# A four-tap filter as diagonal matrix products, a new channel map, and a list scheduler that looks no operation ahead, in one fused two-layer kernel

## The chip, the cores and the metric

The kernel runs on one core of a Trainium2 chip. The metric is the device time of one execution in microseconds (us); less is better.

The engines are named as in the profile: PE is TensorE (matrix products; PEld is its loading of stationary operands), DVE is VectorE, ACT is ScalarE, POOL is GpSimd, SP is the engine that issues the transfers. L562 is line 562 of the kernel in question; the two kernels have different line numbers, so this table goes with all the profiles below:

| work | line before | line after |
|---|---|---|
| transposes of the convolution kernel h | L542 | L546 |
| transposes of k, and diagonal products | none | L561, L578 |
| first stage of the transform | L562 | L599 |
| second stage | L574 | L613 |
| inverse transform, two stages | L596, L608 | L636, L651 |
| MLP: input transposes, up, down products | L774, L787, L804 | L840, L853, L870 |
| evictions from PSUM on ACT, on DVE | L511, L512 | L519, L520 |
| elementwise products and sums on DVE | L501 | L509 |
| normalization on DVE, on ACT | L738, none | L799, L798 |

## The reference

Sequence length S = 2048, D = 512 channels, MLP width 1376, bfloat16.

```
def A(q, k, v, shift_k, ssm_k, ssm_D):
    k_shift[s, d] = sum over t of k_pad[s + t, d] * shift_k[d, 3 - t]     # 4 taps, causal
    kv = k_shift * v
    y  = causal convolution of kv with ssm_k, per channel, length 2048    # by FFT in the reference
    y  = y + kv * ssm_D
    return q * y
def B(x): return gelu(layernorm(x) @ w1 + b1) @ w2 + b2

x = q
x = x + A(layernorm(x), k, v, ...);  x = x + B(layernorm(x))
x = x + A(layernorm(x), k, v, ...);  x = x + B(layernorm(x))
```

The convolution y depends on k, v and the coefficients only, so it is computed once for both layers. What is left of each layer is pointwise products, normalizations and an MLP.

## The kernel before

The convolution is done by TensorE as a two-stage transform (products with constant matrices), pointwise products on VectorE, and a two-stage inverse. It is done in two halves of 1024 positions. Between them and behind them eight MLP blocks of 512 positions run, four of which (layers 1 and 2 of positions 0 to 1023) need only the first half of the convolution; the last four need the second half. So MLP matmuls of the first four blocks are the filler that keeps TensorE busy during the second half of the convolution.

Once in the first half and twice in the second, two transfers of 1 MB each exchange partitions 0 to 63 of an array in SBUF with partitions 64 to 127. Such a pair is called a swap below; the VectorE products that follow need it.

Everything is recorded as operations with estimated durations, and a list scheduler fixes each engine's order when the kernel is built (code is shortened here and below):

```
for e in free:                              # each engine
    ...
    first = min(got)                        # the op that can start earliest
    lim = first[0] + (self.LOOK * d if e != SP else 0.0)      # LOOK = 0.6; d: duration of first
    x = min((x for x in got if x[0] <= lim), key=...)         # the most urgent op that can start by lim
```

With LOOK = 0.6 an engine may pass over an operation that is ready and leave itself idle for up to 0.6 of that operation's duration, for one of higher priority.

The filter on VectorE, four times in each half, each operation on 128 partitions x 1024 elements:

```
def shift(w, hf):
    for j in range(3): tap(3 - j, t[j])             # multiply by a coefficient row
    tt(t[1], t[0], t[1], ALU.add); tap(0, t[0]); tt(t[2], t[1], t[2], ALU.add); tt(t[1], t[2], t[0], ALU.add)
    v = A(0, 128, VV[hf] + w * 16, [512, 8], [64, 8], [1, 16])
    tt(v, t[1], v, ALU.mult)
```

The first stage of the transform takes slices of k*v as stationary operand, 128 rows by 64 columns, with 64 elements between columns (`co = 64`); for h the columns lie side by side (`co = 1`):

```
stage1([(R_H0, 64, 1, 256)], C1, 0, range(8))                     # h:   go = 64, co = 1
stage1([(VV[0], 1, 64, 0)], R_SX, 0, range(2 * w, 2 * w + 2))     # k*v: go = 1,  co = 64
...
ins.append((ri, i, j, A(0, 128, o + (8 * d8 + i) * go, [co, 64]), A(0, 128, R_F + fo + 128 * ri, [1, 128])))
```

In an access pattern such as `[co, 64]` the first number is the step in elements, the second the count.

Of the kernel before, what the change touches and what calls it, by code (L numbers as in the profile page):

```python
# [40 lines left out]
class Op:  # L41
    __slots__ = ("i", "engs", "eng", "fn", "dur", "preds", "succ", "prio", "tile", "dma", "start", "end",
                 "pos", "inc", "waits", "val", "npred", "ready", "bytes", "base", "extra")


class Prog:
# [6 lines left out]
    LOOK = 0.6  # L53
# [130 lines left out]
    def schedule(self):  # L184
        ops = self.ops
        n = len(ops)
# [17 lines left out]
        free = {e: 0.0 for e in (PE, ACT, DVE, POOL, SP)}  # L204
# [9 lines left out]
        while done < n:  # L214
            best = None
            for e in free:
                te = max(free[e], 0.0)
                got = []
                for o in ready[e]:
                    if o.eng is not None:  # L220
                        continue
                    s = max(te, o.ready)
                    new = [x for x in o.tile if x.base is None]
                    if new:
                        pl = self._place(new, s)
                        if pl is None:
                            continue
                        s = pl[0]
                    got.append((s, -o.prio, o.i, o))
                cand = None  # L230
                if got:
                    first = min(got)
                    d = first[3].dur if isinstance(first[3].dur, (int, float)) else first[3].dur[e]
                    lim = first[0] + (self.LOOK * d if e != SP else 0.0)
                    x = min((x for x in got if x[0] <= lim), key=lambda x: (x[1], x[0], x[2]))
                    cand = (x[:3], x[3])
                if cand is None:
                    continue
                o = cand[1]
                d = o.dur if isinstance(o.dur, (int, float)) else o.dur[e]  # L240
                if best is None or (cand[0][0], cand[0][0] + d) < best[0]:
                    best = ((cand[0][0], cand[0][0] + d), e, o, cand[0][0])
# [18 lines left out]
            if o.dma:  # L261
                dma_free = max(dma_free, s + d) + o.bytes / 370.0
                o.end = dma_free + 1900.0
            else:
                o.end = s + d
# [168 lines left out]
def bass_interleave_layers__ssm_conv_h3__mixer_channel_mlp__prompt_kernel(  # L434
# [3 lines left out]
    NS = 192  # L438
# [26 lines left out]
    R_ID, R_F, R_D, R_B1, R_U, R_T2, R_SJ = (place(n) for n in (128, 512, 16, 16, 256, 2048, 2048))  # L465
# [7 lines left out]
    R_SX = R_XT  # L473
    R_SR = R_HT + 7168 - 2048
    HR = C6
    HT1 = C6 + 4096
    TM = [C6 + 4096, C4 + 4096]
    VV = [R_V, C4]
    XS = [R_X0 + s * 512 for s in range(8)] + [R_K + s * 512 for s in range(8)]
    YS = [R_V + s * 512 for s in range(8)] + [C3 + s * 512 for s in range(8)]  # L480
    M_B1, M_ST, M_MV, M_RS, M_HF = 0, 16, 16 + 96, 16 + 96 + 32, 16 + 96 + 32 + 16
# [37 lines left out]
    def load_h(hf):  # L519
        dma(A(0, 128, HR, [1024, 4], [1, 1024]), dr(A_ssm_k, hf * B, [2048, 128], [128 * 2048, 4], [1, 1024]), 1 << 20)  # L520

    def load_kv(hf):
        if hf == 0:
            dma(A(64, 64, R_K, [1, 1536]), dr(A_k, (8 * 64 - 3) * 512, [8 * 512, 64], [1, 1536]), 3 << 16)
            dma(A(1, 63, R_K, [1, 1536]), dr(A_k, 5 * 512, [8 * 512, 63], [1, 1536]), 3 << 16)
        else:
            dma(A(0, 128, R_K, [1, 1536]), dr(A_k, (B - 3) * 512, [8 * 512, 128], [1, 1536]), 3 << 17)
        dma(A(0, 128, R_K + 1536, [1, 4096]), dr(A_k, hf * B * 512, [8 * 512, 128], [1, 4096]), 1 << 20)
        dma(A(0, 128, VV[hf], [1, 4096]), dr(A_v, hf * B * 512, [8 * 512, 128], [1, 4096]), 1 << 20)
# [4 lines left out]
    def turn_h(hf, dst0):  # L534

        for a2 in range(2):
            tl = Tile(cv[hf], 0, hi[hf])
            ins = [(i * 512 + b * 128, A(0, 128, HR + b * 1024 + 4 * a2 + i, [8, 128])) for i in range(4) for b in range(4)]

            def f(e, ins=ins, tl=tl):  # L540
                for o, src in ins:
# [3 lines left out]
            evac(A(0, 128, dst0 + a2 * 32, [64, 64], [8, 4], [1, 8]),  # L545
                 lambda tl=tl: QB(tl, 0, 128, 0, [1, 64], [512, 4], [64, 8]), tl, dur={ACT: 1790.0, DVE: 2200.0})  # L546

    def stage1(terms, s, hf, d8s, engs=None):


        for d8 in d8s:
            tl = Tile(cv[hf], 0, hi[hf])
            ins = []
            for i in range(8):
                for j, (o, go, co, fo) in enumerate(terms):
                    for ri in range(2):
                        ins.append((ri, i, j, A(0, 128, o + (8 * d8 + i) * go, [co, 64]),
# [9 lines left out]
    def stage2(s, dst0, hf, g, engs=None):  # L567

        tl = Tile(cv[hf], 0, hi[hf])
        ins = [(i, A(0, 128, R_S2 + (16 * g + i) * 128, [1, 128]), A(0, 128, s + (16 * g + i) * 64, [1, 64])) for i in range(16)]  # L570

        def f(e):
            for i, w, m in ins:
                r = e.matmul(Q(tl, 0, 128, i * 64, [1, 64]), w, m, start=True, stop=True)  # L574
            return r
        P.op(PE, f, 16 * 29.0, reads=[x for y in ins for x in y[1:]], tile=tl)
        evac(A(0, 128, dst0 + 16 * g, [128, 64], [1, 16]), lambda: Q(tl, 0, 128, 0, [1, 64], [64, 16]), tl, engs)

    def swap(dst0, src0):
        for h in range(2):  # L580
            s = A(64 * h, 64, src0, [1, 8192])
            o = dma(A(64 - 64 * h, 64, dst0, [1, 8192]), s, 1 << 20, reads=[s])
        return o

    def G32(r, g):
        return A(0, 128, r + 32 * g, [128, 64], [1, 32])

    def inverse(p1, p2, z, y, hf):
        for d8 in range(8):
# [4 lines left out]
            def f(e, ins=ins, tl=tl):  # L594
                for i, j, w, m in ins:
# [3 lines left out]
            evac(A(0, 128, z + 8 * d8, [512, 16], [64, 8], [1, 8]),  # L599
                 lambda tl=tl: Q(tl, 0, 128, 0, [8, 16], [1, 8], [128, 8]), tl)  # L600
        for a2 in range(4):
            tl = Tile(cv[hf], 0, hi[hf])
            ins = [(i, ri, A(0, 128, R_T2 + ((2 * a2 + i) * 2 + ri) * 128, [1, 128]),
                    A(0, 128, z + ((2 * a2 + i) * 2 + ri) * 512, [1, 512])) for i in range(2) for ri in range(2)]

            def f(e, ins=ins, tl=tl):
                for i, ri, w, m in ins:
                    r = e.matmul(Q(tl, 0, 128, i * 512, [1, 512]), w, m, start=ri == 0, stop=ri == 1)  # L608
                return r
            P.op(PE, f, 4 * 216.0, reads=[x for y_ in ins for x in y_[2:]], tile=tl)  # L610
            evac(A(0, 128, y + a2 * 1024, [1, 1024]), lambda tl=tl: Q(tl, 0, 128, 0, [1, 1024]), tl)

    def shift(w, hf):  # L613

        t = [A(0, 128, TM[hf] + 1024 * i, [128, 8], [16, 8], [1, 16]) for i in range(3)]

        def tap(j, o):
            tt(o, A(0, 128, R_K + (3 - j) * 512 + w * 16, [512, 8], [64, 8], [1, 16]),
               A(0, 128, R_SJ + j * 512 + w * 16, [0, 8], [64, 8], [1, 16]), ALU.mult, 600.0)
# [6 lines left out]
        v = A(0, 128, VV[hf] + w * 16, [512, 8], [64, 8], [1, 16])  # L626
        tt(v, t[1], v, ALU.mult, 600.0)
# [4 lines left out]
    z = A(0, 1, R_K, [1, 1536])  # L632
    P.op(POOL, lambda e, z=z: e.memset(z, 0.0), 1300.0, writes=[z])
    tload(t_sm, row, 0, R_ID, 640)
    dma(A(0, 128, R_D, [1, 4]), dr(A_ssm_D, 0, [1, 128], [128, 4]), 1024)
    load_h(0)  # L636
    dma(A(0, 128, R_SR, [1, 2048]), dr(A_shift_k, 0, [0, 128], [1, 2048]), 1 << 19)
    load_kv(0)
# [4 lines left out]
    d0, dd = A(0, 128, HR, [1024, 4]), A(0, 128, R_D, [1, 4])  # L643
    P.op(POOL, lambda e: e.tensor_tensor(d0, d0, dd, ALU.add), 600.0, reads=[d0, dd], writes=[d0])
    for j in range(4):
        o, i = A(0, 128, R_SJ + 512 * j, [1, 512]), A(0, 128, R_SR + j, [4, 512])

        def f(e, o=o, i=i):
            if e is nc.scalar:
                return e.activation(o, i, AF.Copy)  # L650
            return e.tensor_copy(o, i)  # L651
        P.op((ACT, DVE), f, {ACT: 520.0, DVE: 600.0}, reads=[i], writes=[o])
    turn_h(0, R_H0)
    stage1([(R_H0, 64, 1, 256)], C1, 0, range(8))
# [9 lines left out]
    for w in range(4):  # L664
        shift(w, 0)
        stage1([(VV[0], 1, 64, 0)], R_SX, 0, range(2 * w, 2 * w + 2))
    for g in range(8):
        stage2(R_SX, C5, 0, g)
        if g % 2:
            tt(G32(C1, g // 2), G32(C5, g // 2), G32(C3, g // 2), ALU.mult, 1100.0)  # L670
            tt(G32(C4, g // 2), G32(C5, g // 2), G32(C4, g // 2), ALU.mult, 1100.0)
    inverse(C1, C4, R_SX, YS[0], 0)
# [4 lines left out]
    load_kv_late = load_kv  # L677
    load_h(1)
    load_kv_late(1)
    turn_h(1, HT1)  # L680
    stage1([(R_H0, 64, 1, 0), (HT1, 64, 1, 256)], C1, 1, range(8))
    for g in range(8):
        stage2(C1, C6, 1, g)
    for w in range(4):
        shift(w, 1)
        stage1([(VV[1], 1, 64, 0)], C1, 1, range(2 * w, 2 * w + 2))
# [13 lines left out]
    inverse(C6, C4, C1, YS[8], 1)  # L700
# [15 lines left out]
    def stats(sl, double):  # L716
# [13 lines left out]
        P.op(POOL, lambda e: e.tensor_scalar(v, v, m1, a1, ALU.mult, ALU.add), 220.0, reads=[v], writes=[v])  # L730
        h = M(0, 128, M_HF, [1, n])
        P.op(POOL, lambda e: e.tensor_tensor(r, v, h, ALU.pow), 1060.0, reads=[v, h], writes=[r])  # L732
        return [(M(0, 128, mv + 2 * i, [1, 1]), M(0, 128, M_RS + 4 * k + i, [1, 1])) for i in range(n)]

    def norm(s, mr, o):
        x = A(0, 128, XS[s], [1, 512])
        m, r = mr
        P.op(DVE, lambda e: e.tensor_scalar(o, x, m, r, ALU.subtract, ALU.mult), 350.0, reads=[x, m, r], writes=[o])  # L738
# [13 lines left out]
    for L, b in [(0, 0), (0, 1), (1, 0), (1, 1), (0, 2), (0, 3), (1, 2), (1, 3)]:  # L752
        lo = 2 if b < 2 else 0
        P.boost = {PE: 1e6, ACT: 2e6, DVE: 2e6, POOL: 2e6} if b < 2 else {}
        sl = list(range(4 * b, 4 * b + 4))
        mr = stats(sl, False)
# [6 lines left out]
        mr = stats(sl, True)  # L763
        k = blk[0]
        blk[0] += 1
# [79 lines left out]
```

## Time and profile before

302.0 us (median of four runs, 301.85 to 302.98). The profiled execution, one that took 300.4 us, has a span of 298.3 us at a mean granted TensorE clock of 0.949.

| | first half's convolution, 0 to 72.9 us | the rest, 72.9 to 298.3 us |
|---|---|---|
| TensorE busy | 43.5 us (60%) | 206.5 us (92%) |
| VectorE busy | 56.8 us | 149.9 us |
| granted clock | 0.86 | 0.98 |

I cut at the last eviction of the first half's inverse. The page first: busy totals, and the span in 40 equal slices (a digit is the busy share in tenths; PEclk is the granted clock in tenths).

```profile
PE 250.0 (84%) x2336; PEld 143.4 (48%) x2336; DVE 206.6 (69%) x407; ACT 155.4 (52%) x194; POOL 27.1 (9%) x43
...
PE   0788580795999999979899959995999999899995
...
PEclk9999756699999999999999997999699999999999
```

The stretches of the table, as the windows view of the kernel before gives them (length; busy of PE, PEld, DVE, ACT, POOL with instruction counts; clock; DMA share; GB/s):

```profile
0.00:72.90 72.90, 43.51 (x721) 39.23 (x722) 56.76 (x88) 41.57 (x41) 6.40 (x15) 0.86 0.77 255
72.90:298.30 225.40, 206.50 (x1616) 104.17 (x1616) 149.85 (x320) 113.83 (x153) 20.70 (x28) 0.98 0.13 34
```

The chain that ended last, its pieces in the first half (start, duration, what):

```profile
13.90 12.02 ACT ar L511 x13
...
30.07 2.41 DVE ar L501 x4
32.51 1.30 DVE ar L501 x2
...
45.18 9.17 DVE ar L501 x8
54.40 7.85 PE ps L596 x112
```

Read: evictions on ScalarE, then filter operations on VectorE, then eight VectorE products for which the whole inverse (L596) waits, TensorE idle. After that TensorE bounds the kernel.

TensorE's timeline just after the second half's inverse has ended at 200.0 us (the bracket is the idle time before the piece, and what ended it):

```profile
199.86 4.05 PE L804 MATMUL ps<-ar 128*128 128x512 bf16 x18
207.59 1.97 PE L774 MATMUL ps<-ar 128*128 128x128 bf16 x16 [3.67 <-DVE ar L738]
210.25 9.30 PE L787 MATMUL ps<-ar 128*128 128x512 bf16 x32 [0.69 <-ACT ar L511]
```

TensorE runs out of filler (L804), waits 3.7 us for the normalization that feeds the fifth MLP block, and then does 32 matmuls in 9.30 us; the same group takes 7.35 us at 254.5 us (granted clock 0.78 and 1.00 in the windows view of the two). This point, where the filler of the first four blocks ends and the fifth block begins, is called the handover below.

### The profile page before, as it was taken

How to read it: one execution, taken by the hardware profiler on the slowest of the kernel's cores; microseconds unless marked ns; L12 is line 12 of the kernel's file. 1: busy time of each engine (PE TensorE's matmuls, PEld its weight loads, DVE VectorE, ACT ScalarE, POOL GpSimd, SP SyncE). 2: the span in 40 equal slices, each digit the busy share in tenths (PEclk: the TensorE clock that was granted, in tenths of full speed). 3: DMA queues.
4: the chain of work that ended last, by engine and by line, in shares of the span. 5: the costliest groups of instructions: out<-in, count | busy, mean ns of one | idle time of the engine just before them, and what ended most of it. 6: DMA issues, size and time to landing. Idle time of an engine off the chain costs nothing.

```text
span 298.3 us, 5439 instructions
## 1 busy us (share of the span) xinstructions
PE 250.0 (84%) x2336; PEld 143.4 (48%) x2336; DVE 206.6 (69%) x407; ACT 155.4 (52%) x194; POOL 27.1 (9%) x43
## 2 busy tenths in 40 slices
PE   0788580795999999979899959995999999899995
PEld 0687570774855755344445424742335444344342
DVE  0699869799889936689889698749714777841031
ACT  1599542258899663552757231770451641654510
POOL 2100000221020000120220000301100110110000
PEclk9999756699999999999999997999699999999999
DMA  6997899730000059100005901000000000001001
GB/s 221 396 416 320 178 242 303 278 141 2 3 2 2 5 172 217 32 0 2 0 0 108 200 11 37 35 2 36 0 0 2 0 0 2 1 0 35 2 35 70
DMA packets 8753, 26.19 MB, mean 88 GB/s; under 512 B 2490, under 2 KB 3995, under 8 KB 7066
## 3 DMA queue, kind: packets, MB, share of 16 engines
q1 hardware_dynamic: 8730, 25.86, 28.1%
q8 instruction: 18, 0.29, 0.4%
q14 instruction: 5, 0.04, 0.0%
HBM read 17.47 MB, written 2.10 MB: 66 GB/s over the span
## 4 chain that ended last, share of the span: by engine, by line
PE 53%; DVE 18%; ACT 13%; DMA 10%; POOL 3%; issue 1%; SPq 1%; DVEq 0%
PE ps L804 17%; PE ps L787 17%; ACT ar L511 12%; DVE ar L501 10%; DMA ar<-ar 8%; PE ps L562 6%; PE ps L596 4%; PE ps L574 3%; DVE sm L724 3%; PE ps L774 2%; DVE ar L808 2%; PE ps L608 2%; DMA ar<-in_A_ssm_k_dram 2%; POOL sm L732 2%; DVE ar L738 2%; PE ps L542 2%
## 5 line engine op out<-in xcount | busy, mean ns | idle before, releaser
L511 ACT ACTIVATE ar<-ps 128x1024 bf16<-128x1024 f32 (+2 forms) x103 | 94.1, 969 | 70.9 <-PE ps L774 31.2
L501 DVE TENSOR_TENSOR ar<-ar 128x512 bf16<-128x512 bf16 (+2 forms) x160 | 102.8, 685 | 14.6 <-DMA ar<-ar 6.2
L792 ACT ACTIVATE ar<-ps,sm 128x512 bf16<-128x512 f32 (+1 forms) x88 | 60.4, 687 | 51.3 <-PE ps L787 51.0
L787 PE MATMUL ps<-ar 128*128 128x512 bf16 (+1 forms) x352 | 84.3, 387 | 3.2 <-ACT ar L511 2.1
L804 PE MATMUL ps<-ar 128*128 128x512 bf16 (+1 forms) x352 | 82.4, 385 | 3.9 <-DVE ar L808 3.9
L804 PEld LDWEIGHTS ps<-ar 128*128 128x128 bf16 (+1 forms) x352 | 33.0, 99 | 46.2 <-DVE ar L808 4.9
L787 PEld LDWEIGHTS ps<-ar 128*128 128x128 bf16 (+1 forms) x352 | 31.2, 101 | 48.9 <-ACT ar L792 15.1
L808 DVE TENSOR_TENSOR ar<-ar,ps 128x512 bf16<-128x512 bf16 x32 | 21.2, 685 | 43.2 <-PE ps L804 43.1
L724 DVE BATCH_NORM_STATS2 sm<-ar 128x6 f32<-128x512 bf16 x64 | 41.3, 681 | 0.0
L562 PE MATMUL ps<-ar 128*64 128x128 bf16 x640 | 31.4, 260 | 9.5 <-ACT ar L511 6.0
L562 PEld LDWEIGHTS ps<-ar 128*64 128x64 bf16 x640 | 29.1, 160 | 12.5 <-ACT ar L511 5.1
L738 DVE TENSOR_SCALAR ar<-ar,sm 128x512 bf16<-128x512 bf16 x64 | 23.0, 406 | 11.5 <-POOL sm L732 11.2
L730 POOL TENSOR_SCALAR sm<-sm 128x4 f32<-128x4 f32 x16 | 5.7, 357 | 224.8 <-DVE sm L726 224.8
L596 PE MATMUL ps<-ar 128*128 128x128 bf16 x256 | 16.9, 230 | 9.9 <-DVE ar L501 9.5
L574 PE MATMUL ps<-ar 128*128 128x64 bf16 x512 | 20.9, 202 | 5.0 <-ACT ar L511 2.9
L574 PEld LDWEIGHTS ps<-ar 128*128 128x128 bf16 x512 | 18.8, 104 | 10.9 <-ACT ar L511 7.2
L596 PEld LDWEIGHTS ps<-ar 128*128 128x128 bf16 x256 | 15.9, 104 | 11.2 <-DVE ar L501 9.6
L732 POOL TENSOR_TENSOR sm<-sm 128x4 f32<-128x4 f32 x16 | 18.1, 1130 | 1.3
L512 DVE CAST ar<-ps 128x1024 bf16<-128x1024 f32 x9 | 11.0, 1225 | 5.9 <-PE ps L574 2.5
L774 PE MATMUL ps<-ar 128*128 128x128 bf16 x128 | 10.4, 231 | 4.2 <-DVE ar L738 3.8
L542 PE MATMUL ps<-ar 128*128 128x128 bf16 x64 | 6.0, 269 | 8.7 <-DMA ar<-in_A_ssm_k_dram 7.1
L774 PEld LDWEIGHTS ps<-ar 128*128 128x128 bf16 x128 | 8.2, 103 | 7.2 <-DVE ar L738 5.0
(17 smaller groups left out, 38.6 us busy)
## 6 DMA issues: line engine op xcount, KB each, us to landing
ar<-ar SPq DMA_DIRECT2D x6, 1024.0 KB, 9.2
ar<-tab_s SPq DMA_DIRECT2D x4, 1024.0 KB, 16.1
ar<-in_A_ssm_k_dram SPq DMA_DIRECT2D x2, 1024.0 KB, 7.5
ar<-in_A_k_dram SPq DMA_DIRECT2D x2, 1024.0 KB, 8.3
ar<-in_A_v_dram SPq DMA_DIRECT2D x2, 1024.0 KB, 7.7
ar<-in_A_q_dram SPq DMA_DIRECT2D x2, 1024.0 KB, 13.4
out_dram<-ar SPq DMA_DIRECT2D x8, 256.0 KB, 2.2
ar<-in_B_w_dram SPq DMA_DIRECT2D x1, 1376.0 KB, 15.7
```

The lines of the kernel that those rows point to most:

```text
L501: return P.op(eng, lambda e: e.tensor_tensor(o, a, b, op), dur, reads=[a, b], writes=[o])
L511: return e.activation(dst, src(), AF.Copy)
L562: r = e.matmul(Q(tl, 64 * ri, 64, i * 128, [1, 128]), w, m, start=j == 0, stop=j == len(terms) - 1)
L574: r = e.matmul(Q(tl, 0, 128, i * 64, [1, 64]), w, m, start=True, stop=True)
L596: r = e.matmul(Q(tl, 0, 128, i * 128, [1, 128]), w, m, start=j == 0, stop=j == 1)
L724: P.op(DVE, lambda e, st=st, x=x: e.bn_stats(st, x), 630.0, reads=[x], writes=[st])
L738: P.op(DVE, lambda e: e.tensor_scalar(o, x, m, r, ALU.subtract, ALU.mult), 350.0, reads=[x, m, r], writes=[o])
L774: r = e.transpose(QB(tl, 0, 128, 128 * j, [1, 128]), src[j], IDN)
L787: r = e.matmul(Q(tl, 0, rows, 0, [1, 512]), w, m, start=dk == 0, stop=dk == 3)
L792: P.op(ACT, lambda e, dst=dst, tl=tl, rows=rows, bias=bias: e.activation(dst, Q(tl, 0, rows, 0, [1, 512]), AF.Gelu_apprx_tanh, bias=bias), ...
L804: r = e.matmul(Q(tl, 0, 128, 0, [1, 512]), ins[fc][0], ins[fc][1], start=fc == 0, stop=fc == 10)
L808: P.op(DVE, lambda e, x=x, tl=tl: e.tensor_tensor(x, x, Q(tl, 0, 128, 0, [1, 512]), ALU.add), 620.0, reads=[x], writes=[x], tile=tl)
```

## The change

Its intent is a shorter first half. Six parts come together:

- (a) In the first half, TensorE does the filter. It transposes k, and multiplies the shifted transposes by diagonal matrices of the coefficients, so that the product comes out in the original layout. VectorE only multiplies the result by v, out of PSUM.
- (b) The channel map is d = 8 g + j. Each group's 64 columns now lie side by side, so every stationary operand of the first stage is contiguous.
- (c) The first half's products and inverse are cut into two halves of channels, so that one half's inverse can run beside the other half's products. The second stage of k*v then runs as 256 matmuls of 32 columns.
- (d) The scheduler: LOOK is 0; a rule (PEN = 300) gives an operation that ScalarE or VectorE could do to VectorE only if ScalarE would be clearly later; two constants of its model change.
- (e) The MLP: normalizations may run on ScalarE (27 of 64 do), the second statistics of a block are computed for pairs, and earlier blocks get priority over later ones.
- (f) Loads: k first, in two pieces; the coefficients' spread for the second half moves to GpSimd.

```diff
-    LOOK = 0.6
+    LOOK = 0.0
+    PEN = 300.0
@@ scheduler
+                    if len(o.engs) == 2 and e == DVE:
+                        q = max(free[ACT], o.ready) + sum(... durations of more urgent ops ready for ACT ...)
+                        if q + o.dur[ACT] <= s + o.dur[DVE] + self.PEN:
+                            continue
@@ new: filter on TensorE, per block b of 128 channels
+        for a in range(8):
+            for j in range(4):
+                o = R_KT + (b * 8 + (a - j) % 8) * 132 + (2 if a >= j else 1)
+                ins.append((a, j, A(0, 128, o, [1, 128]), A(0, 128, R_DG + (b * 4 + j) * 128, [1, 128])))
+        ...     r = e.matmul(Q(tl, 0, 128, a * 128, [1, 128]), w, m, start=j == 0, stop=j == 3)
+        v = A(0, 128, VV[0] + b * 128, [512, 8], [8, 16], [1, 8])
+        o = A(0, 128, KV[0] + b * 1024, [8, 8], [64, 16], [1, 8])
+        P.op(DVE, lambda e: e.tensor_tensor(o, Q(tl, 0, 128, 0, [128, 8], [8, 16], [1, 8]), v, ALU.mult), ...)
@@ stage1
-                for j, (o, go, co, fo) in enumerate(terms):
-                        ins.append((ri, i, j, A(0, 128, o + (8 * d8 + i) * go, [co, 64]),
+                for j, (o, fo) in enumerate(terms):
+                        ins.append((ri, i, j, A(0, 128, o + (8 * d8 + i) * 64, [1, 64]),
@@ first half
-    for w in range(4):
-        shift(w, 0)
-        stage1([(VV[0], 1, 64, 0)], R_SX, 0, range(2 * w, 2 * w + 2))
-    for g in range(8): stage2(R_SX, C5, 0, g) ... products ...
-    inverse(C1, C4, R_SX, YS[0], 0)
+    stage1([(KV[0], 0)], R_SX, 0, range(8))
+    for u in range(2):
+        for g in range(4): stage2(R_SX, C5, 0, g, 32 * u, 32) ... products ...
+        inverse1(C1, C4, C6, 0, range(4 * u, 4 * u + 4))
+        inverse2(C6, YS[0], 0, 256 * u, 256)
@@ MLP
-        P.boost = {PE: 1e6, ACT: 2e6, DVE: 2e6, POOL: 2e6} if b < 2 else {}
+        first = (1e6, 2e6) if b < 2 else (0.0, 0.0)
+        P.boost = {e: first[e != PE] - 5e4 * k for e in (PE, ACT, DVE, POOL)}
-        mr = stats(sl, True)
+        mr = stats(sl[:2], True, k > 0) + stats(sl[2:], True, k > 0)
         ... (norm: DVE only before; ACT or DVE after)
```

## The prediction

> **What bounds the kernel now.** The table by stretches of the span (298.3 us) shows two regimes. Up to 72.9 us, the first half's convolution, TensorE is busy 43.5 us only. After that it is busy 206.5 of 225.4 us: TensorE-bound, with 19 us of holes. In the first regime the chain of waits runs through ScalarE's evictions (13.9 to 27 us, 1.03 us each), then VectorE filter multiplies (30 to 35 us), stage-2 evictions, eight VectorE products (45.2 to 54.4 us, TensorE and ScalarE idle) and the inverse transform (54.4 to 72.9 us). VectorE cannot evict from 12.7 to 35 us, because it runs 32 filter operations of 0.65 us (20.9 us in the timeline). TensorE's granted clock averages 0.64 from 30 to 55 us; [...] 128 stage-2 matmuls took 6.1 us there, against about 4.2 at full clock.
>
> **Removed.** The 32 filter operations on VectorE (20.9 us); the wait of the whole inverse for all eight products: channels now go in two halves, so the inverse of one overlaps the products of the other.
>
> **Added.** On TensorE, estimated from full-clock durations in the trace: 32 transposes (74 to 113 ns each, about 3 us), 128 diagonal matmuls (57 ns each in the second half's inverse, 7.3 us), and twice as many stage-2 matmuls for the k*v branch (33 ns each, so +4.2 us). On VectorE four multiplies out of PSUM (about 1.2 us each, like its 1.225 us evictions) and four diagonal builds (0.4 us). Eight short evictions.
>
> **New first half.** k lands near 6.5 us and TensorE starts before h is there; stage 1 starts near 12 us. TensorE then needs 5.6 + 7.3 + 4.2 + 5.6 + 8.4 = 31 us, so the inverse starts near 44. The new instruction order gives all its twelve evictions to ScalarE: 12 x 1.03 plus latency, so the first half ends near 58 us instead of 73.
>
> **The rest.** The second half's first transposes (2.4 us), done before 72.9 us today, move behind that point, so about 13 of the 15 us reach the end. The later part stays TensorE-bound. Some normalizations move to ScalarE (25-odd of 64 in the order), statistics come in pairs, and fewer holes should remain: I expect 3 to 5 of 19 us of holes, and of the two late clock dips (32 matmuls in 9.3 instead of 7.1 us at 210 us), to go.
>
> Predicted: 286 us (279 to 293). Faster by over 2%: 0.96; within 2%: 0.03; slower: 0.01.
>
> **What would show it.** Right: no vector filter operations in the first 45 us; first inverse matmul near 44 us, last first-half eviction near 58; granted clock near 1 from 15 to 55 us; TensorE busy about 260 us (250 + 14.5 - 4 from the clock). Holes after the first half: 14 to 16 us. Wrong: a gap before the first-half products, waiting for the partition-swap transfer (it must land by about 42 us); the clock still low; diagonal matmuls at over 70 ns.
>
> **What would make it wrong.** Evictions of the new layouts not at 1.03 us; the swap delayed by loads on the same queue; the scheduler's new order leaving TensorE without filler while second-half swaps (11.5 us each) run, which would give back 5 us; or filling the late holes better than I expect, which would bring 278 us.

The sum is 302 - 15 for the first part (58 for 73 us) - about 1 for the rest (2.4 us of transposes added, 3 to 5 us of holes taken off) = 286. That the clock of the new first half would be near 1 stands as my estimate, as does the line "- 4 from the clock", which is 6.1 - 4.2 and 9.3 - 7.1. The 4.2 and the 7.1 are estimates too, 128 matmuls at 33 ns and 32 at 0.22 us, from the matmuls of before at a clock of 1.00; measured there, a group of 32 takes 7.25 to 7.35 us.

## More of the kernel before

The group of first-stage matmuls (busy us, mean ns of one from start to end, idle before):

```profile
L562 PE MATMUL ps<-ar 128*64 128x128 bf16 x640 | 31.4, 260 | 9.5 <-ACT ar L511 6.0 <-DVE ar L501 3.3
```

## The result, and the profile after

277.2 us (median of four runs, 275.87 to 278.78). A ratio here is the mean time of one kernel's fast runs over the mean of the other's of the same rounds, so not quite the ratio of the medians: 0.9175, 95% interval 0.9112 to 0.9237. The direction was right; the time lies below the range of 279 to 293.

The profiled execution has a span of 277.0 us at a clock of 0.974. The same page lines and windows for the kernel after, cut at its own last first-half eviction, 62.9 us:

```profile
PE 244.4 (88%) x2640; PEld 144.8 (52%) x2640; DVE 183.4 (66%) x360; ACT 170.1 (61%) x221; POOL 45.6 (16%) x106
...
PE   0997953896999999988899899989999999989995
...
PEclk9999977899999999999799999999999999999999
```

```profile
0.00:62.90 62.90, 45.70 (x1006) 42.84 (x1007) 40.24 (x54) 38.77 (x42) 8.04 (x20) 0.92 0.88 290
62.90:277.00 214.10, 198.74 (x1637) 101.92 (x1635) 143.17 (x306) 131.38 (x179) 37.52 (x86) 0.99 0.14 35
```

So the span lost 21.3 us: 10.0 in the first part, where I had expected 15, and 11.3 in the rest, where I had expected about 1. TensorE has 304 instructions more and is busy 5.6 us *less*. In the rest, its busy time fell by 7.8 us and its idle time by 3.5 us (225.4 - 206.5 = 18.9, 214.1 - 198.7 = 15.4).

Over the whole kernel the busy time fell mainly in one group, the first stage, from 31.4 to 21.2 us. The new filter group and VectorE's product out of PSUM are beside it:

```profile
L599 PE MATMUL ps<-ar 128*64 128x128 bf16 x640 | 21.2, 220 | 2.9 <-ACT ar L519 2.8
...
L578 PE MATMUL ps<-ar 128*128 128x128 bf16 x128 | 8.0, 219 | 0.2 <-issue 0.2
...
L583 DVE TENSOR_TENSOR ar<-ps,ar 128x1024 bf16<-128x1024 f32 x4 | 4.9, 1225 | 7.5 <-PE ps L578 7.5
```

TensorE's waits, the two longest (line, what it waited for: us in total, times, longest), and its timeline in the first part:

```profile
PE ps L613 <- issue: 9.1, 3, 5.4
PE ps L561 <- DMA ar<-in_A_k_dram: 6.3, 1, 6.3
```

```profile
29.79 4.22 PE L599 MATMUL ps<-ar 128*64 128x128 bf16 x128
34.03 0.84 PE L613 MATMUL ps<-ar 128*128 128x32 bf16 x27
37.13 3.55 PE L613 MATMUL ps<-ar 128*128 128x32 bf16 x128 [2.25 <-issue]
46.06 2.88 PE L613 MATMUL ps<-ar 128*128 128x32 bf16 x101 [5.38 <-issue]
49.37 0.90 PE L636 MATMUL ps<-ar 128*128 128x128 bf16 x7 [0.43 <-issue]
```

The wait for the VectorE products, 9.5 us before, is gone. In its place stand holes that end at nothing the profile shows ("issue"): no operand, no semaphore, no buffer. The two long ones here fall in the middle of one uniform group of matmuls.

And the end of the second half's inverse (L651, over at 179.0 us), to be held against the three lines at 200 us of before:

```profile
178.80 1.89 PE L853 MATMUL ps<-ar 128*128 128x512 bf16 x8
181.98 6.23 PE L870 MATMUL ps<-ar 128*128 128x512 bf16 x28 [1.28 <-ACT ar L858]
188.05 1.06 PE L840 MATMUL ps<-ar 128*128 128x128 bf16 x16
189.70 2.50 PE L853 MATMUL ps<-ar 128*128 128x512 bf16 x10 [0.60 <-DVE ar L520]
```

Here 36 MLP matmuls are left to do while VectorE prepares the fifth block (35 of them start after the inverse has ended), and the block's transposes (L840) start without a hole. The same 16 transposes take 1.06 us, against 1.97 in before (clock 1.00 and 0.50 in the windows view).

### The profile page after: what moved, and what is told of

Read it like the earlier page. It is cut to its first block, busy times and chain, and to the rows that moved or that the text cites. A ratio compares the mean times of both kernels' runs of the same rounds, so it can differ in the third digit from the quotient of the medians.

```text
span 277.0 us, 6100 instructions
## 1 busy us (share of the span) xinstructions
PE 244.4 (88%) x2640; PEld 144.8 (52%) x2640; DVE 183.4 (66%) x360; ACT 170.1 (61%) x221; POOL 45.6 (16%) x106
## 4 chain that ended last, share of the span: by engine, by line
PE 61%; DVE 14%; ACT 9%; DMA 7%; issue 5%; POOL 2%; SPq 1%
PE ps L870 23%; PE ps L853 22%; ACT ar L519 6%; PE ps L613 5%; DVE ar L509 5%; DMA ar<-ar 5%; PE ps L636 4%; DVE ar L874 4%; PE ps L578 3%; DMA ar<-in_A_ssm_k_dram 3%; PE ps L599 2%; DVE ar L520 2%; DVE sm L776 2%; ACT ar L858 2%; ACT ar L798 1%
## 5 line engine op out<-in xcount | busy, mean ns | idle before, releaser
L509 DVE TENSOR_TENSOR ar<-ar 128x512 bf16<-128x512 bf16 (+2 forms) x132 | 85.1, 687 | 28.3 <-ACT ar L519 15.5
L858 ACT ACTIVATE ar<-ps,sm 128x512 bf16<-128x512 f32 (+1 forms) x88 | 59.2, 687 | 30.1 <-PE ps L853 29.8
L874 DVE TENSOR_TENSOR ar<-ar,ps 128x512 bf16<-128x512 bf16 x32 | 21.2, 685 | 38.1 <-PE ps L870 38.1
L782 POOL TENSOR_SCALAR sm<-sm 128x2 f32<-128x2 f32 (+1 forms) x24 | 7.9, 328 | 142.9 <-DVE sm L778 142.4
L613 PE MATMUL ps<-ar 128*128 128x64 bf16 (+1 forms) x640 | 21.5, 190 | 9.1 <-issue 9.1
L798 ACT ACTIVATE ar<-ar,sm 128x512 bf16<-128x512 bf16 x27 | 21.3, 811 | 4.7 <-POOL sm L789 4.7
L599 PE MATMUL ps<-ar 128*64 128x128 bf16 x640 | 21.2, 220 | 2.9 <-ACT ar L519 2.8
L799 DVE TENSOR_SCALAR ar<-ar,sm 128x512 bf16<-128x512 bf16 x37 | 14.4, 430 | 12.2 <-POOL sm L789 11.8
L599 PEld LDWEIGHTS ps<-ar 128*64 128x64 bf16 x640 | 18.4, 110 | 6.7 <-ACT ar L519 4.2
L787 POOL TENSOR_TENSOR sm<-sm 128x2 f32<-128x2 f32 (+1 forms) x24 | 21.4, 893 | 2.0
L636 PE MATMUL ps<-ar 128*128 128x128 bf16 x256 | 16.3, 225 | 0.7 <-issue 0.4
L520 DVE COPY ar<-ps 128x512 bf16<-128x512 bf16 (+1 forms) x20 | 9.6, 501 | 4.3 <-PE ps L561 2.4
L840 PE MATMUL ps<-ar 128*128 128x128 bf16 x128 | 9.6, 220 | 1.0 <-DVE ar L874 0.7
L840 PEld LDWEIGHTS ps<-ar 128*128 128x128 bf16 x128 | 7.8, 98 | 4.1 <-DVE ar L874 0.8
```

What stands on the lines that cost most here:

```text
L509: return P.op(eng, lambda e: e.tensor_tensor(o, a, b, op), dur, reads=[a, b], writes=[o])
L599: r = e.matmul(Q(tl, 64 * ri, 64, i * 128, [1, 128]), w, m, start=j == 0, stop=j == len(terms) - 1)
L613: r = e.matmul(Q(tl, 0, 128, i * nd, [1, nd]), w, m, start=True, stop=True)
L636: r = e.matmul(Q(tl, 0, 128, i * 128, [1, 128]), w, m, start=j == 0, stop=j == 1)
L787: P.op(POOL, lambda e: e.tensor_tensor(r, v, h, ALU.pow), 1060.0, reads=[v, h], writes=[r])
L798: return e.activation(o, x, AF.Identity, bias=mr[2], scale=mr[1])
```

## The experiments

Sixteen kernels ran. "After" and "before" are the two kernels above; times are medians, ratios are to the runs of before on the same chip in the same rounds. Theories:

- **T1**, mine at the start: the parts act where the prediction put them; what I missed in the rest is the first stage's contiguous operand.
- **R1**: the scheduler's order alone brings the gain, and the new operations little.
- **R2**: the filter and the channel halves bring nearly everything, the order little.

| kernel | us | ratio to before, 95% |
|---|---|---|
| sched_on_before | 301.2 | 0.998 (0.992 to 1.004) |
| order_mlp_on_before | 306.9 | 1.018 (1.013 to 1.023) |
| sched_off_after | 305.3 | 1.013 (1.009 to 1.017) |
| look_only | 306.0 | 1.013 (1.009 to 1.017) |
| look_pe | 290.7 | 0.962 (0.957 to 0.967) |
| look_dve | 297.8 | 0.984 (0.978 to 0.990) |
| pen_off | 293.7 | 0.971 (0.967 to 0.976) |
| norm_dve | 285.8 | 0.947 (0.941 to 0.953) |
| nosplit | 285.4 | 0.946 (0.940 to 0.953) |
| taps_dve | 283.9 | 0.942 (0.937 to 0.947) |
| strided_both | 298.6 | 0.993 (0.986 to 1.000) |
| strided_runs | 282.0 | 0.933 (0.929 to 0.937) |
| late_w | 276.6 | 0.914 (0.910 to 0.918) |
| late_w_again | 275.3 | 0.913 (0.909 to 0.917) |
| after_again | 276.4 | 0.916 (0.911 to 0.921) |
| tiny_swap (wrong result, one run) | 271.9 | none |

### Order or operations? sched_on_before, order_mlp_on_before, sched_off_after

The first puts part (d) alone on the kernel before, the second (d) and (e); the third takes (d) out of the kernel after.

```diff
sched_on_before, on before           sched_off_after, on after
-    LOOK = 0.6                      -    LOOK = 0.0
+    LOOK = 0.0                      -    PEN = 300.0
+    PEN = 300.0                     +    LOOK = 0.6
+ the rule for ScalarE/VectorE       - the rule
+ constants 700 and 400              + constants 0 and 370
```

> The kernel before with only the list scheduler's new rules (no look-ahead, ScalarE preferred for shared evictions, start and transfer constants). Theory 1 (the gain is in the work, not the order): the first half's chain still runs through 32 vector filter operations, so the time stays within 3 us of before, 299 to 303 us, and the last first-half eviction stays at 70 us or later. Rival (the new order is what fills the holes): 292 us or less, with holes on TensorE after the first half falling from 18.9 to under 14 us.

> The changed kernel with the old scheduler rules. Theory 1: 278 to 282 us, so at most 4 us of the 25 are the order's. Rival: 286 us or more.

> The kernel before with everything of the change that is not in the convolution: all scheduler rules, normalizations that may run on ScalarE, statistics in pairs, the priority of earlier MLP blocks. The changed kernel with the old rules took 305 us and the kernel before with the new rules 301 us, so either needs the other. If what is missing lies in the convolution's own operations (TensorE filter, map, halves): 296 to 304 us. If it lies in the MLP's operations: 285 us or less. In both cases the end of the second half's inverse plus 97 to 101 us gives the span, as in all ten runs so far.

Measured: with the operations of before, the new order gives 301.2 us against 301.5 for before in its rounds; with the MLP parts as well 306.9. With the operations of after and the old order 305.3. Only both together give 277.2. So neither R1 nor R2 holds: of the 25 us, none can be given to either alone. (306.9 lies above both ranges that I had written down for order_mlp_on_before.)

On before's operations the new order did shorten the rest (224.2 us from the end of the first half's inverse to the end, where before has 230.1) and lengthened the first part by more (that inverse ended at 75.9 us instead of 68.2). Why the first part lengthened I did not trace further. With the old order on after's operations, TensorE's busy time stays at 249.5 us even with a few records missing, five more than in after, and its holes over 0.15 us sum to 49.4 us against 28.8.

### Which part of the order? look_only, look_pe, look_dve, pen_off

All four are the kernel after with one thing put back: LOOK = 0.6 for all engines, for TensorE's list alone, for VectorE's list alone; or the ScalarE rule taken out.

```diff
look_only:  -    LOOK = 0.0
            +    LOOK = 0.6
look_pe:    -  lim = first[0] + (self.LOOK * d if e != SP else 0.0)
            +  lim = first[0] + (0.6 * d if e == PE else 0.0)
look_dve:   +  lim = first[0] + (0.6 * d if e == DVE else 0.0)
pen_off:    -  if len(o.engs) == 2 and e == DVE: ... continue      (the rule)
```

> The changed kernel with the old look-ahead of 0.6 of an operation's duration, all other rules new. The changed kernel with all old rules took 305 us: the eight first-half products stood in one block behind evictions, and the second half's second swap was issued at 163 us instead of 131 us. If the look-ahead is what does it: 298 to 306 us and the second swap issued after 155 us. If it is the rule that keeps shared evictions on ScalarE: 275 to 281 us.

> The changed kernel without the rule that keeps shared evictions and normalizations on ScalarE unless VectorE would be well ahead; no look-ahead, as in the change. If the look-ahead is what does it: 276 to 282 us. If the ScalarE rule does it: 295 us or more.

> The changed kernel with the old look-ahead of 0.6 of an operation on TensorE's list alone. With look-ahead on all engines it took 306 us, with 47 holes of 0.15 to 2 us (22 us) against 24 (15 us). If the loss is TensorE leaving ready filler matmuls for a more urgent operation that comes later than planned: 292 us or more. If it is VectorE's and ScalarE's order: 277 to 286 us.

> The changed kernel with the old look-ahead on VectorE's list alone. If VectorE's order (products kept behind more urgent MLP operations that are not yet ready) is what lengthens the second half's chain: 290 us or more, and the second half's inverse ends at 190 us or later. If it is TensorE's look-ahead: 277 to 284 us.

Measured, above after's 277.2: look-ahead on every list +29 us, on TensorE's alone +13, on VectorE's alone +21, the rule out +17. The parts do not add up. All four leave the operations as they are, so this is order alone. look_only and look_dve came as one of the two theories written down for each had it; look_pe (292 or more) and pen_off (295 or more) fell just short of theirs.

Where it goes is seen in two places. One is many small holes: TensorE has 47 holes of 0.15 to 2 us in look_only (22.3 us), 44 in look_pe (19.2 us) and 24 in after (14.9 us), counted in the traces. The other is the point at which the second half's inverse ends. These are TensorE's two longest waits in look_only; the second, 8.1 us, is the input transposes (L840) waiting for a normalization, which after's waits have with 0.2 us only:

```profile
PE ps L613 <- issue: 8.8, 3, 5.2
PE ps L840 <- DVE ar L799: 8.1, 3, 5.3
```

And TensorE's timeline in pen_off, where the last MLP matmuls (L864) run among the inverse's (L645):

```profile
190.25 1.89 PE L645 MATMUL ps<-ar 128*128 128x512 bf16 x8
191.97 0.81 PE L864 MATMUL ps<-ar 128*128 128x512 bf16 x3
200.50 1.89 PE L834 MATMUL ps<-ar 128*128 128x128 bf16 x16 [7.72 <-DVE ar L793]
203.08 10.12 PE L847 MATMUL ps<-ar 128*128 128x512 bf16 x32 [0.69 <-ACT ar L513]
```

The filler is spent when the inverse ends. TensorE waits 7.7 us for the fifth block's normalization, and afterwards runs at a reduced clock: the window view of pen_off has 0.70 from 200.5 to 215 us and 1.00 behind that. A second loss follows the hole: 32 matmuls take 10.1 us instead of the 7.35 seen in before at a clock of 1.00. That the hole is what brings the clock down is not shown by a run of its own. Counted over the traces in which all 704 MLP matmuls were recorded:

| kernel | MLP matmuls of the first four blocks that start after the second inverse has ended | longest hole after it, us |
|---|---|---|
| after, strided_runs, nosplit, late_w | 35 | 1.3 |
| before | 17 | 3.7 |
| look_only | 5 | 5.3 |
| pen_off, norm_dve, order_mlp_on_before | 2 | 7.7, 7.0, 7.7 |

look_dve (8.1 us), sched_off_after (5.4) and sched_on_before (6.6) show the hole too, but some matmul records are missing from their traces, so they are not counted. look_pe does not have it there; it loses by a 4.4 us hole at 110 us and by small ones. So one thing that most losing orders share is shown: filler used up before the handover to the fifth block. What is not shown by an experiment of its own is how much of each loss it makes. In pen_off the hole, less after's 1.3, and the slower 32 matmuls come to 6.4 + 2.8 = 9.2 of 16.5 us.

The hole is not the whole of it, for the traces show a rival to this reading. From the end of the second half's inverse to the end of the span, before takes 98.3 us, after 98.0, look_only 99.0, norm_dve 98.8 and pen_off 100.9 (look_pe alone is far from this, 106.6): a kernel that has used up its filler has less left to do, and the hole stands in its place. By this count the time is lost before the handover: that inverse ends at 179.0 us in after, 185.7 in norm_dve, 192.1 in pen_off, 195.0 in look_dve, 200.0 in before and 206.4 in look_only. The work that leads up to it runs late too: from the landing of the second half's first swap to the issue of its second, while its VectorE products run, after takes 14.5 us, norm_dve 18.0, pen_off, look_dve and look_only about 27 and before 38.0. The expectation of look_dve had named this chain, with an end of the inverse at 190 us or later as its mark, and the mark was met. But this stretch alone does not set the time: taps_dve has 26.6 us there and nosplit 25.0, and they lose 6.7 and 8.3. Either a late chain used up the filler, or an order that spent the filler early left the hole; no run separates the two, so the cause inside the order stays open.

### Normalizations on ScalarE, statistics in pairs: norm_dve

```diff
-        mr = stats(sl, False, k > 0)
+        mr = stats(sl, False, False)
-        mr = stats(sl[:2], True, k > 0) + stats(sl[2:], True, k > 0)
+        mr = stats(sl, True, False)
```

> The changed kernel with all normalizations on VectorE and statistics in fours, as before; filter, map, halves and scheduler stay. If relief of VectorE is what lets the eight products after the second half's first swap run at once (15.6 us from its landing to the second swap's issue, against 38.4 us before): 283 to 290 us and that stretch over 22 us. If it is the order alone: 276 to 280 us, stretch under 20 us.

Measured: 285.8 us, 8.6 more than after. What I expected between the second half's two swaps did not come: from the landing of the first to the issue of the second it took about 18 us. The hole is at the handover again:

```profile
185.57 0.81 PE L870 MATMUL ps<-ar 128*128 128x512 bf16 x3
193.37 1.98 PE L840 MATMUL ps<-ar 128*128 128x128 bf16 x16 [6.98 <-DVE ar L799]
196.03 10.09 PE L853 MATMUL ps<-ar 128*128 128x512 bf16 x32 [0.69 <-ACT ar L519]
```

7.0 us of hole and 10.09 - 7.35 = 2.7 us of slower matmuls (clock 0.76 from 194 to 210 us) are 9.7 us, against after's 1.3 us hole: 8.4 us, where the profiled span grew by 7.6 and the median by 8.6. That the part pays by keeping VectorE from being what TensorE waits for at this one point fits these lines, but is not shown: as said above, the inverse also ended 6.7 us later than in after.

### The two halves of channels: nosplit

```diff
-    for u in range(2):
-        for g in range(4): stage2(R_SX, C5, 0, g, 32 * u, 32) ...
-        inverse1(C1, C4, C6, 0, range(4 * u, 4 * u + 4)); inverse2(C6, YS[0], 0, 256 * u, 256)
+    for g in range(8): stage2(R_SX, C5, 0, g) ...
+    inverse1(C1, C4, C6, 0, range(8)); inverse2(C6, YS[0], 0)
```

> The changed kernel without the two channel halves in the first half: stage 2 of k*v in 64-column matmuls (128 instead of 256), all eight products, then the whole inverse. Theory: without the overlap the inverse starts 2 to 4 us later, but 128 fewer instruction pairs take one 16 KB block and its wait away, so the first half's inverse ends within 3 us of 61.6 us; 277 to 283 us. Rival (the halves are worth what the prediction thought): 284 us or more.

Measured: 285.4 us, 8.3 more than after, so the rival that put it at 284 or more was right. The wait that part (c) was meant to take away is back, one hole in TensorE's timeline:

```profile
51.40 9.48 PE L636 MATMUL ps<-ar 128*128 128x128 bf16 x128 [11.22 <-DVE ar L509]
```

The first half's inverse ends at 65.7 us instead of 61.6. That is as much as half of the 8.3 us. A hole of 4.3 us at 124.8 us, which after does not have, is as large as the other half; where it comes from I did not trace.

### The filter back on VectorE: taps_dve

This is the kernel after with the filter of the first half on VectorE, in the new layout (`shift(w, 0)` in place of the transposes and the diagonal products, with before's order of loads, and the coefficients' spread back on ScalarE and VectorE; so part (f) is undone with it).

> The changed kernel with the first half's filter back on VectorE (32 vector operations, k with its halo rows, no transposes of k, no diagonal matmuls); channel map, halves, scheduler and normalizations stay. Theory 1 (the filter on TensorE is worth about the 10 us by which the first half ended earlier, less what the map gives): 282 to 287 us, last first-half eviction at 67 to 71 us. Rival (the split into channel halves and the map gave nearly all of it): under 280 us.

Measured: 283.9 us, 6.7 more than after. TensorE waits for the filter in two places:

```profile
34.42 1.92 PE L599 MATMUL ps<-ar 128*64 128x128 bf16 x32 [4.54 <-DVE ar L509]
...
40.08 1.92 PE L599 MATMUL ps<-ar 128*64 128x128 bf16 x32 [3.74 <-DVE ar L509]
```

Yet the first half's inverse ends only 1.9 us later, at 63.5 us, and its last eviction at 64.7, where I had expected 67 to 71. In after the diagonal products end sooner, and the time goes into the holes without a cause at 35 and 41 us. So taking out the part for which the change is named, with (f), costs 6.7 us of the 25, and only 1.9 of it in the part it was meant for.

### The contiguous stationary operand: strided_both, strided_runs

Both give the first stage of k*v a stationary operand with 64 elements between columns again, as in before, and have VectorE write k*v in that layout.

```diff
-   A(0, 128, o + (8 * d8 + i) * 64, [1, 64])
+   A(0, 128, o + (8 * d8 + i) * go, [co, 64])       # k*v: go, co = 1, 64
strided_both: -  o = A(0, 128, KV[0] + b * 1024, [8, 8], [64, 16], [1, 8])
              +  o = A(0, 128, KV[0] + b * 16, [512, 8], [1, 16], [64, 8])     # neighbours 64 apart
strided_runs: +  o = A(0, 128, KV[0] + b * 16, [512, 8], [64, 8], [1, 16])     # runs of 16; its inputs are read with a step of 8
```

> The changed kernel, the order of all engines unchanged; only the filtered product k*v is stored so that the 64 columns of the stationary operand of its stage-1 matmuls lie 64 elements apart, as before, instead of side by side. Theory 1 (the channel map pays by contiguous weight loads): those 256 matmuls go from about 31 to about 66 ns, TensorE is busy 8 to 9 us longer, the second half's 4.5 us reach the end whole and the first half's in part: 282 to 286 us. Rival (the 66 ns were the clock's or the interleaving's doing, the map only rearranges): 276 to 279 us.

> Repeats the strided test without its fault: in the first one VectorE's scattered writes took 4.86 us each instead of 1.2. Here the product is written in runs of 16 elements; the stationary columns still lie 64 elements apart, the order of all engines is that of the changed kernel. Theory 1 (the map pays by contiguous weight loads): stage-1 matmuls of k*v at about 66 instead of 31 ns, TensorE busy 8 to 9 us longer in sum, time 281 to 286 us. Rival (the 21 us of the first test were VectorE's writes alone): 279 us or less.

strided_both came to 298.6 us, but it tells little of TensorE: VectorE's writes with 64 elements from each to the next cost 4.9 us each, not 1.2 (this line is its product out of PSUM, after's is shown above with a mean of 1225 ns):

```profile
L583 DVE TENSOR_TENSOR ar<-ps,ar 128x1024 bf16<-128x1024 f32 x4 | 18.7, 4857 | 5.1 <-PE ps L578 5.1
```

I had made the experiment without thinking of the writer. strided_runs mends most of that: VectorE writes in runs of 16 elements and reads every eighth, and the instruction order of every engine is that of after. It took 282.0 us, 4.8 more than after:

```profile
L602 PE MATMUL ps<-ar 128*64 128x128 bf16 x640 | 29.8, 248 | 3.4 <-ACT ar L519 2.5 <-DVE ar L877 0.6 <-DVE ar L520 0.3
...
L583 DVE TENSOR_TENSOR ar<-ps,ar 128x1024 bf16<-128x1024 f32 x4 | 8.1, 2027 | 4.7 <-PE ps L578 4.7
```

```profile
30.02 8.12 PE L602 MATMUL ps<-ar 128*64 128x128 bf16 x128
```

The same 128 matmuls took 4.22 us in after: 63 ns against 33 ns each. The group goes back to 29.8 us from 21.2, of before's 31.4. VectorE's products still cost 2.0 instead of 1.2 us, so not all of the 4.8 us is TensorE's, but the 8.6 us of matmul time is. TensorE's whole busy time rose by 5.6 us only (250.0 against 244.4): 2.5 of the 3.0 us between are two groups that ran at a reduced clock in after, the first 80 matmuls of the inverse (5.61 us at 0.84; 4.78 here) and 32 at 133.2 us (8.89 us at 0.81; 7.26 here). The mean clock is 0.994 here against 0.974. T1's missing term is shown. T1's other half, that the parts act where the prediction put them, is not borne out: taken out one at a time they cost 29 us (look_only), 17 (pen_off), 8.6 (norm_dve), 8.3 (nosplit) and 6.7 (taps_dve), far more than 25 in sum.

In the rest of the kernel the first stage took 16.8 us in before, 13.0 in after and 17.7 here. The windows view, of these matmuls alone (length; busy of PE and PEld; clock; DMA share; GB/s), first before, then after:

```profile
72.90:298.30 225.40, 16.82 (x384) 15.46 (x384) 0.98 0.13 34
62.90:277.00 214.10, 13.03 (x384) 11.09 (x384) 0.99 0.14 35
```

The remaining 1.6 of the 10.2 us saved are not the stride's: h's first 128 matmuls, contiguous in both kernels, took 5.57 us in before and 3.97 in after. Why is not shown; in after TensorE had started on k before them.

The number of columns is 64 in both layouts, and the time per matmul with its load still goes from 33 to 63 ns. For VectorE's product out of PSUM the three layouts measured are: 1.225 us with reads and writes in runs of 8 elements, 2.027 us with reads that step by 8 and writes in runs of 16, and 4.857 us with reads in runs of 8 and every element written 64 from the last.

### The holes without a cause: late_w, tiny_swap, after_again, late_w_again

What the trace of after shows: the holes that end at nothing stand after TensorE's 221st, 348th, 603rd and 731st matmul, 127, 255 and 128 apart. (A fifth, of 0.43 us after the 832nd, stands where a new group begins and does not fit the step.) The page's line for the instruction queue has 20 packets, 0.33 MB in all, 16 KB each. TensorE resumes 1.3 to 1.6 us after such a packet has landed: packets that land at 35.55 and 44.73 us, matmuls again at 37.13 and 46.06. In quiet stretches a packet starts when TensorE is at about the 85th matmul of a block of 128; up to 49 us it starts some 48 to 134 matmuls later than that, and the three long holes come where it is 106, 130 and 134. The packet itself takes 0.9 to 1.0 us before these holes, and 0.9 to 1.5 elsewhere: it starts late, it is not slow. That a packet feeds about 128 matmuls with their loads, a block, is my estimate from these distances and from the pages: 2640 matmuls, as many loads and 20 packets in after, 2336 and 18 in before, and 19 packets in nosplit, which has 128 matmuls fewer than after. The three long holes cost TensorE 9.1 us; from 34.9 to 49.4 us, where two of them end, the share of the DMA engines is 0.95. The theory: the packets queue behind the large transfers of the first half. late_w takes load from that time, moving the MLP weights behind the second half's v; tiny_swap does so as well, and cuts the first partition swap (2 MB within SBUF) to 1/16, with the rest of its target cleared by GpSimd, so its result is wrong.

```diff
late_w:     the three loads of w1 and w2 placed behind the load of v in SP's list; nothing else moved
tiny_swap:  the same, and
-   o = dma(A(64 - 64 * h, 64, dst0, [1, 8192]), A(64 * h, 64, src0, [1, 8192]))
+   o = dma_start(A(64 - 64 * h, 64, dst0, [1, 512]), A(64 * h, 64, src0, [1, 512]))
```

> The changed kernel, the order of all compute engines unchanged; only the loads of the two MLP weights (2.8 MB) go behind the second half's loads on the transfer queue, so they no longer run beside the first swap. Theory (TensorE's 5.4 us hole at 40.7 us, and the 2.3 us one at 34.9 us, are waits for 16 KB blocks of its own instructions, which queue behind bulk transfers): the swap lands at 35 to 39 instead of 42.7 us, the two holes together fall under 4 us, the first half ends 3 to 5 us earlier and the time is 271 to 275 us. Rival (the hole is a wait on data or on PSUM that the profile does not show): the hole stays at 5 us and the time within 1 us of 277.

> Wrong results on purpose: the late weight loads, and the first swap moves 1/16 of its bytes (the rest of its target is set to zero beforehand), so the transfer queues are nearly idle from 31 us until the second half's loads. With the loads late the two holes of TensorE were 2.3 and 3.8 us, and TensorE went on 1.3 to 1.4 us after its next 16 KB block had landed. If those holes are instruction blocks queued behind the swap: each falls under 1.7 us and the blocks start within 1 us of TensorE running out. If they wait on data or PSUM instead: they stay above 2 and 3 us.

> The changed kernel once more, beside the late loads on one chip: 275 to 279 us.

> The late weight loads once more, beside the changed kernel on one chip. The holes measured before say 2 to 2.5 us less than the changed kernel (first-half inverse ends at 59.1 instead of 61.6 us); if nothing of it reaches the end, within 0.8 us of it.

late_w: 276.6 us, where I had expected 271 to 275. Its holes summed to 7.2 instead of 9.1 us, and the swap landed no earlier (43.1 us), where I had expected 35 to 39. From the issue of its second transfer a 2 MB swap took 11.4 to 13.3 us to land in all these runs (about 160 to 180 GB/s), in the second half as well. tiny_swap: the hole at 35 us is gone; the second is shorter, not short:

```profile
34.01 4.04 PE L613 MATMUL ps<-ar 128*128 128x32 bf16 x155
41.06 2.87 PE L613 MATMUL ps<-ar 128*128 128x32 bf16 x101 [3.01 <-issue]
```

I had expected each under 1.7 us; its block started at 38.7 us, with other large loads under way. Then the repeats: after_again had no hole at 35 us either, and 4.7 us at 38; late_w_again had none at 35 and 6.0 at 39, longer than any in after. So the holes vary from one execution to the next by as much as the experiment moved them. late_w and its repeat are 0.6 and 1.0 us faster than after's runs beside it or earlier, which the intervals cover; no version that clearly beats the kernel after was found. What the trace shows is that TensorE resumes 1.3 to 1.6 us after a late packet of the instruction queue has landed; that the large transfers make the packets late is not shown: tiny_swap has the smallest sum of these holes (4.3 us), but it is one execution, and after_again, with nothing changed, has 6.1 in the same group.

## Why the prediction was wrong

I predicted 286 us and measured 277.2. The direction, faster, was right; the range was not.

**The step that failed is "The rest": "The later part stays TensorE-bound", costed at about -1 us.** It did stay TensorE-bound and it was worth -11.3 us. Of that, the holes shrank by 3.5 us, which is what I had written ("3 to 5 of 19 us"). The term of the sum that was missing is TensorE's own work. I took it to be fixed, but for 2.4 us of transposes moved in. It fell by 7.8 us:

- The first stage in this part took 13.0 instead of 16.8 us. I had read the new channel map as a change of address only and gave it no cost. In the timeline of before, 32 matmuls of L562 took 1.08 us with h (first line) and 2.20 with k*v (second), at a clock of 1.00 in both; that the stride of 64 was the difference stood in the diff. strided_runs shows it.

```profile
79.59 1.08 PE L562 MATMUL ps<-ar 128*64 128x128 bf16 x32
107.56 2.20 PE L562 MATMUL ps<-ar 128*64 128x128 bf16 x32
```

- Fewer stretches at a reduced clock. I had written that part of "the two late clock dips" would go. Of the two (16 matmuls in 5.31 us at 178.9 us, clock 0.68; 32 in 9.30 at 210.3, clock 0.78), neither is there after; one new one is (32 in 8.89 us at 133.2, clock 0.81). Against the same groups at a clock of 1.00 (16 in 3.62 us, 32 in 7.35, 16 transposes in 1.06) the dips cost 4.6 us in before (with 16 transposes in 1.97) and 1.5 in after, so 3.0 us net.

The two make 6.8 us. With 1.3 us of transposes moved in (I had 2.4), 9.0 us have to be explained; the other 2.2 us are not assigned.

For the same two reasons "TensorE busy about 260 us" failed, at 244.4. The added work was near or below its cost: 8.0 us for the diagonal products (7.3 predicted), 3.6 for the transposes of k (3), and only 0.9 more for the second stage of the first part (11.8 us against 10.9, predicted +4.2), whose 32-column matmuls took 28 ns each (128 in 3.55 us). Part of that is luck: before's 128 matmuls for k*v ran at a clock of 0.60 and took 6.12 us. Against the 4.2 us of my estimate (128 at 33 ns), after's 256 took 7.3, 3.1 more. What was taken away, 10.2 us of first stage, I had at zero.

**"New first half" was too good by 5 us.** The inverse began at 49.4 us, predicted 44, and the last eviction ended at 62.9, predicted 58. The matmuls in it were not slower than costed; the 9.1 us of holes that end after a late instruction packet were in none of my terms. The list of TensorE's waits in before has none of them; near those times TensorE waited for VectorE there (3.35 us up to 35.3, 1.33 up to 38.8, 9.46 up to 54.4). With these holes in it, the stretch from 34.9 to 49.4 us had a clock of 0.71, where I had said near 1. That it would be near 1 without idle windows was my estimate. In these traces long holes and a low clock often stand together: here; in before, 3.67 us of hole at the handover and then 0.76 (207.6 to 222 us); in pen_off 7.7 us and then 0.70, in norm_dve 7.0 us and then 0.76. Not always: after's 1.28 us of hole at 182.0 us is followed by 1.00, and its stretch at 0.81 at 133.2 us has only 0.87 us of idle time right before it. That idle time brings the low clock is not shown by a run of its own. My assumption that the idle windows would be gone failed in any case.

**Two small terms.** I had taken the time of a run to be 3.7 us above its span; in the profiled run it was 1.8. And that run was itself 1.6 us above the median. The sum closes: 10.2 us too much in the rest, 4.9 too little in the first part, 1.9 and 1.6 for these, make the 8.8 us. That the first two have opposite signs is luck; without the first part's error the forecast would have been off by 14 us.

**Right**: no VectorE filter operations in the first half; diagonal products at 56 ns (one group of 32 starts at 25.19 us and the next piece at 26.98); the eviction-like product out of PSUM at 1.225 us; all twelve inverse evictions on ScalarE; the swap landing at 42.7 us, in time; 15.4 us of holes after the first half (14 to 16 predicted). The risk that I named last, "filling the late holes better than I expect, which would bring 278 us", is not what happened, though the time came close to its 278: the late holes were as I expected. Where the risk lies, though, the experiments show that the order decides (35 matmuls of filler left, or 2), and I did not follow the order far enough to count the filler.

## What to carry to other kernels

Price a change of layout on every engine that reads or writes it: a stationary operand with a stride cost a factor of 1.9 here (63 against 33 ns per matmul), scattered writes on VectorE a factor of 4.0 (4.857 against 1.225 us), and undoing the first was worth more TensorE time (8.6 us in strided_runs) than the added products cost (8.0). In a TensorE-bound kernel with an order fixed at build, look at each handover where the filler ends and the next block's input must be ready; in before, pen_off, norm_dve and look_only a hole there (3.7, 7.7, 7.0 and 5.3 us) was followed by slower matmuls (32 in 9.3 to 10.1 us, not 7.35). Then ask what used up the filler, a late chain or an early order. And do not divide a gain among parts that were only tried together: here the order alone gave nothing, the operations alone lost 4 us, and both gave 25.
